# Earlier query projections in layer 1, a later memset and cycling tail banks in a two-layer attention and token-mixer kernel

## The chip, the cores and the metric

The kernel runs on one core of a Trainium2 chip. The metric is device time in microseconds (us) of one execution. A core has a matrix engine (TensorE, PE; its weight loads are shown as PEld), VectorE (DVE), ScalarE (ACT), GpSimd (POOL) and a queue engine (SyncE, SP), which run their own instruction lists in order and wait for each other through semaphores. Matrix results land in eight PSUM banks; everything else lives in SBUF.

## What is computed

Two layers, each an attention block and a token-mixing MLP, with layer normalisation before each and a residual after each, on a sequence of S = 2048 tokens of D = 640 with H = 32 heads of 20, and F = 1536 hidden units that mix along the sequence. Both layers use the same weights.

```python
def _A_ref(x, wqkv, wo):
    B, S, D = x.shape
    H = 32
    Dh = D // H
    qkv = (lambda x, *d: x.transpose(*d))((x @ wqkv).reshape(B, S, 3, H, Dh), 2, 0, 3, 1, 4)
    q, k, v = qkv[0], qkv[1], qkv[2]
    scores = jnp.einsum("bhqd,bhkd->bhqk", q, k) * (Dh ** -0.5)
    p = _softmax(scores, axis=-1)
    o = jnp.einsum("bhqk,bhkd->bhqd", p, v)
    return (lambda x, *d: x.transpose(*d))(o, 0, 2, 1, 3).reshape(B, S, D) @ wo

def _B_ref(x, w1, b1, w2, b2):
    B, S, D = x.shape
    h = _layernorm(x, axis=-1)
    u = jnp.einsum("bsd,sf->bdf", h, w1) + b1
    u = _gelu(u)
    y = jnp.einsum("bdf,fs->bds", u, w2) + b2
    return (lambda x, *d: x.transpose(*d))(y, 0, 2, 1)

x = A_x
x = x + _A_ref(_layernorm(x, axis=-1), A_wqkv, A_wo)
x = x + _B_ref(_layernorm(x, axis=-1), B_w1, B_b1, B_w2, B_b2)
x = x + _A_ref(_layernorm(x, axis=-1), A_wqkv, A_wo)
x = x + _B_ref(_layernorm(x, axis=-1), B_w1, B_b1, B_w2, B_b2)
return x
```

## The kernel before

**Tiling.** Tokens go in 16 tiles of 128 and in four blocks of 512 (`tb` for keys, `qb` for queries). Heads go in eight groups `g` of four. A *unit* is one query block, one head group and one key tile; its four heads are four *chunks* of 128 x 512 scores. A layer has 512 units and 2048 chunks. Scores S = K Q (L703) are written by PE into a 3-bank and a 2-bank PSUM tile in turn, ScalarE takes their exponential (L773, forms of 1536 and 1024 columns) into P, and PE sums P with the values into `acc` (L1326). The value tile `Vaug` holds, for each key tile and head, 20 values and a column of ones that gives the softmax denominator.

**Helping ScalarE.** Some chunks have their exponential taken by VectorE and GpSimd instead (L563, L661, L593, L597, L644, L614, L616), in pairs, through the PSUM bank Dt. In layer 0 this starts early (`ve_early = True`), in layer 1 only once all tokens have been fed in.

**The order.** Python code plans the whole kernel: it keeps model clocks for PE, VectorE and ScalarE (`pem`, `dvm`, `acm`), decides step by step what PE does next, and writes the instructions of PE, VectorE, ScalarE and GpSimd in that order. So a changed priority at one place moves instructions in all that follows. Between score rows PE does *fills* out of a queue sorted by priority, lowest number first (`add_fill`, `next_fill`): T (transposes of a normalised tile, L1225), K and Q projections (L1177), V projections (L1201), y (second matmul of the mixer of the layer before, L1685, in layer 1), O (output projection) and M (first matmul of the mixer, L1068). A fill takes one of the banks `misc` and `Dt`, and is copied or added out by VectorE, or by ScalarE at the very start (the helper lines L366 and L370 to L372). Where there is no fill, PE multiplies zeros (L762). `fed` marks the fills that must be done before the second phase of a layer opens.

**Feeding.** After the four transposes of a token block, `t_fill` queues its K projections (priority `when(g, tb) - 4`) and, for block 0, its Q projections. `EQ` holds the query blocks 0 and 1, whose units may run early, on whatever keys are there. For block 1 the four Q projections of the first four groups are queued after the transposes of that block, at L1247 to L1249. `base[1]` is 16, so that their priorities are 28, 36, 44 and 52.

**Start of layer 0.** `TokenFeed.begin` zeroes the values' padding on ScalarE (`zero_values`), and then submits a VectorE memset of the column of ones (L1546), with the model time `e + 5.0` as its earliest. VectorE meanwhile normalises the first six token tiles (statistics L886 to L893, `veps` L901, a power on GpSimd L903, `h_bf` L907); PE transposes four of them, ScalarE copies them to `hh`, and V, K and Q of block 0 follow.

**End of a layer.** When the last unit's sums are out, the 3-bank and 2-bank score tiles become the accumulators `sums` of the last two token tiles' output: ScalarE puts the residual into them (L955), M fills that have been begun or fit into 1.3 us of model time are done, the last projection is added (L960), and the M fills that are left follow. Their banks come from `tail_alloc`: first misc, then Dt, then the third bank of the first score tile; there is no fourth. Their adds into the hidden rows (L1076) on VectorE are kept in the list `held` once L960 is out, and are forced after statistics of the two tiles (L980 to L993). Then come the two normalised tiles (L995, L999) and the mixer (`mixer_head`: um L1753, its add L1756, GELU L1759, then ya and yb).

Of the kernel before, what the change touches and what calls it, by code (L numbers as in the profile page):

```python
# [25 lines left out]
DH = 20  # L26
# [55 lines left out]
def kernel(  # L82
# [12 lines left out]
    nc = tc.nc  # L95
# [16 lines left out]
    def pe(inst):  # L112
        tc.chain_iter_dep("pe_order", inst.ins)
        return inst
# [77 lines left out]
    Vv = Vaug[:, 0:NKT * H * VW].rearrange("p (k h c) -> p k h c", k=NKT, h=H)  # L192
# [26 lines left out]
    def get_QT(st, qb):  # L219
        if qb not in st.QTq:  # L220
            st.QTq[qb] = qtp.tile([128, NG, 512], BF16, name="QTq")
        return st.QTq[qb]

    def attention(st, x_in_ap, x_mid, uacc_l, feed, feed_stack):
# [10 lines left out]
        def s_tile(w):  # L235
            return pp[f"s{w}"].tile([128, w, 512], F32, name="S")
# [38 lines left out]
        misc = Bank(lambda: pp["misc"].tile([128, 512], F32, name="misc"))  # L275
        Dbank = Bank(lambda: pp["dt"].tile([128, 512], F32, name="Dt"))
# [47 lines left out]
        held = []  # L324
# [38 lines left out]
        def copy_on(eng, out_ap, in_ap, scale=None):  # L363
            if eng is acm:
                if scale is None:
                    nc.scalar.copy(out=out_ap, in_=in_ap)  # L366
                else:
                    nc.scalar.mul(out=out_ap, in_=in_ap, mul=scale)
            elif scale is None:
                nc.vector.tensor_copy(out=out_ap, in_=in_ap)  # L370
            else:
                nc.vector.tensor_scalar_mul(out=out_ap, in0=in_ap, scalar1=scale)  # L372
# [15 lines left out]
        base = [0.0]  # L388
# [782 lines left out]
        def proj_fill(kind, g, tb, prio, ready, gate=None, fed=False):  # L1171
            wpad, key = (wk_pad, ("K", g, tb)) if kind == "K" else (wq_pad, ("Q", tb, g))
            scale = None if kind == "K" else q_scale
            mms = []
            for dt_ in range(NDT):
                def mm(t, dt_=dt_):
                    pe(nc.tensor.matmul(t[:, :], lhsT=wpad[:, dt_, g, :], rhs=hT[:, dt_, tb * 512:(tb + 1) * 512],  # L1177
                                        start=(dt_ == 0), stop=(dt_ == NDT - 1)))
                mms.append(mm)

            def evac(t, end, eng):
                dst = KT[:, g, tb * 512:(tb + 1) * 512] if kind == "K" else get_QT(st, tb)[:, g, :]
                copy_on(eng, dst, t[:, :], scale)

            def after(end):
                kready[key] = end + DVE_TO_PE
            add_fill(key, prio, mms, evac, 512, ready=ready, after=after, act=0.6, gate=gate, fed=fed)
# [26 lines left out]
        def when(g, tb):  # L1214
            return base[tb] + per_g[tb] * g if g < EG else place[(0, g)] + 4.0 * tb

        def t_fill(tt, h_bf, ready, done):
            tb = tt // 4

            def view(t):  # L1220
                return t[:, :].bitcast(BF16)[:, 0:D].rearrange("p (a b) -> p a b", a=NDT)
            mms = []
            for dt_ in range(NDT):
                def mm(t, dt_=dt_):
                    pe(nc.tensor.transpose(view(t)[:, dt_, :], h_bf[:, dt_ * 128:(dt_ + 1) * 128], ident[:]))  # L1225
                    if dt_ == NDT - 1:
                        done()
                mms.append(mm)

            def evac(t, end, eng):  # L1230
                copy_on(eng, hT[:, :, tt * 128:(tt + 1) * 128], view(t))

            def after(end):
                tready[tt] = at = end + DVE_TO_PE
                v_fill(tt, 0, feed.wv_early, when(0, tb) + tt % 4 - 1, at, fed=True,
                       gate=(lambda: len(tready) >= 4) if tb == 0 else None)
                if all(4 * tb + i in tready for i in range(4)):
                    for g in list(range(EG)) + rest:
                        gate = feed.gate_late if g >= EG else None
                        owner = next((qb for qb in EQ if part_at[qb] <= g < part_at[qb] + part_rows), None)  # L1240
                        if owner is not None:
                            gate = lambda owner=owner: feed.gate_late() and not any(qg[0] == owner for qg in early_left)
                        proj_fill("K", g, tb, when(g, tb) - 4, max(at, cx.w_at.get((0, g), at + 1.0)), gate=gate, fed=g < EG)
                        if tb == 0:
                            proj_fill("Q", g, 0, when(g, 0) - 4, max(at, cx.w_at.get((1, g), at + 1.0)),
                                      gate=feed.gate_late if g >= EG else None, fed=g < EG)
                    if tb in EQ and tb > 0:  # L1247
                        for g in range(EG):
                            proj_fill("Q", g, tb, base[tb] + 16.0 + 8.0 * g - 4, at, fed=True)  # L1249
                if len(tready) == NT and NQB > 1:  # L1250
                    enqueue_qproj(1)
            add_fill(("T", tt), when(0, tb) - 6 + 0.1 * (tt % 4), mms, evac, D, ready=ready, after=after, wave=0.1,
                     cells=0.25, cost=0.48, act=0.7, fed=True)

# [158 lines left out]
        cx = Ctx()  # L1413
        cx.w_at = {}
        for k_, v_ in dict(dvm=dvm, acm=acm, pem=pem, Proc=Proc, submit=submit, ln_proc=ln_proc, t_fill=t_fill,
                           add_fill=add_fill, when=when, v_fill=v_fill, proj_fill=proj_fill, enqueue_qproj=enqueue_qproj,
                           kready=kready, vready=vready, base=base, rest=rest, tready=tready, s_start=s_start, KT=KT,
                           Dbank=Dbank, misc=misc, spare=spare, warm_bank=warm_bank, acc_free=acc_free, pe_wave=pe_wave,
# [33 lines left out]
        sums = [s_tile(w)[:].rearrange("p a b -> p (a b)") for w in (3, 2)]  # L1452
        for t in sums:
            zero_wave(t[:, 0:512], True, True)
            zero_wave(t[:, 512:D], True, True, HALF / 2, D - 512)
        tail_banks = [sums[0][:, 1024:1536], None, None]

        def tail_alloc():
            bank = tail_banks.pop()
            return bank if bank is not None else Dbank.alloc() if len(tail_banks) == 1 else misc.alloc()  # L1460
        room = pem["t"] + 1.3
        while fs["cur"] is not None or (fill_queue and pem["t"] < room):
            fill_step(tail_alloc)
# [7 lines left out]
    class TokenFeed:  # L1471
        groups = 4
        early_qbs = (0, 1)
        ve_early = True
        act_helps = True
        act_free = 0.0
        warm_until = 5.6
# [28 lines left out]
        def begin(self, cx):  # L1506
# [36 lines left out]
            def zero_values(e):  # L1543
                nc.scalar.memzero(Vv[:, :, :, DH:VW])
                nc.scalar.memzero(Vv[:, :, 4 * self.groups, 0:32 - VW])
                cx.submit(cx.Proc(2.6, [(0.49, lambda e: nc.vector.memset(Vv[:, :, :, DH:DH + 1], 1.0), 0.0)], e + 5.0))  # L1546
            cx.submit(cx.Proc(1.4, [(1.35, zero_values, -0.06),
                                    (0.2, lambda e: nc.scalar.memzero(Vaug[:, NKT * H * VW:]), -0.06)] +
                              [(1.0, lambda e, i=i: nc.scalar.memzero(pads(i, 1)), -0.06) for i in range(2)],
# [43 lines left out]
    class MixFeed:  # L1593
        groups = 4
        early_qbs = (0, 1)
        ve_early = False
        act_helps = True
        act_free = 0.0
        warm_until = 0.0
# [239 lines left out]
    with ExitStack() as a_stack:  # L1839
# [3 lines left out]
        feed = TokenFeed(feed_stack)  # L1843
        attention(st0, A_x[0], xd[0], uacc[0], feed, feed_stack)
    with ExitStack() as a_stack:
# [3 lines left out]
        feed = MixFeed(feed_stack, xd[0], xd[1], st0.ua)  # L1849
# [33 lines left out]
```

## Time and profile before

| what | us |
|---|---|
| three runs, median (lowest to highest) | 1754.15 (1754.06 to 1754.17) |
| the profiled execution | 1754.05 |
| its span, first to last instruction | 1752.3 |
| ScalarE busy in the span | 1665.0 (95%) |
| PE busy | 1677.7 (96%) |
| VectorE busy | 1534.9 (88%) |
| GpSimd busy | 592.0 (34%) |

The engines' busy shares are close to each other, and PE's includes products of zeros and repeated score matmuls that nothing waits for. The chain that ended last, followed back from the end, has ScalarE with 50% of the span, PE with 25% and issue time with 22%. A view by stage says more than these averages: the two attentions lie at 16 to 817 us and 853 to 1681 us; between them and behind them stand the mixers. A row of a timeline gives start, duration, engine, line, operation, output and input tile, shape and count, and in brackets the idle time of the engine before it with what ended it. Durations of neighbouring instructions of ScalarE and VectorE overlap a little, so that the distance from start to start is what one costs.

### The profile page before, as it was taken

The page shows a single profiled execution, that of the slowest core. Times are in us where ns is not written, and L with a number is a line of the kernel's source. Part 1 is how long each engine was busy: PE and PEld are TensorE (multiplying, and loading weights), DVE is VectorE, ACT ScalarE, POOL GpSimd, SP SyncE. Part 2 cuts the span into 40 slices and gives each one's busy share as a digit, 9 for nine tenths or more (in the row PEclk, how much of TensorE's full clock was granted, in tenths as well). Part 3 has the DMA queues.
Part 4 walks back from the last instruction along what each step waited for, and adds up shares of the span by engine and source line. Part 5 has one row for each costly group of instructions (what it writes and reads, how often), then busy time and mean ns, then how long its engine had stood idle before and what let it go on. Part 6 is the DMA issues. An engine that isn't in the chain of part 4 may idle for free.

```text
span 1752.3 us, 43289 instructions
## 1 busy us (share of the span) xinstructions
PE 1677.7 (96%) x17891; PEld 663.4 (38%) x17891; DVE 1534.9 (88%) x2491; ACT 1665.0 (95%) x1498; POOL 592.0 (34%) x936
## 2 busy tenths in 40 slices
PE   8999999999999999999999999999999999999999
PEld 3333333333333344444434433233333333444455
DVE  7789999999999999998543469999999999999973
ACT  8999999999999999999779999999999999999970
POOL 2243443353544343332000023434434443434310
PEclk9999999999999999999999999999999999999999
DMA  4020000000122010133322100001001220101445
GB/s 117 9 24 10 1 2 2 24 24 2 35 66 82 25 47 3 39 97 97 125 69 75 65 11 1 1 2 43 20 2 61 82 76 6 62 3 40 120 122 178
DMA packets 103014, 81.87 MB, mean 47 GB/s; under 512 B 50976, under 2 KB 87456, under 8 KB 102816
## 3 DMA queue, kind: packets, MB, share of 16 engines
q1 hardware_dynamic: 97280, 71.22, 13.5%
q0 software_dynamic: 5536, 7.88, 1.5%
q8 instruction: 140, 2.29, 0.5%
q14 instruction: 58, 0.48, 0.1%
HBM read 55.48 MB, written 23.59 MB: 45 GB/s over the span
## 4 chain that ended last, share of the span: by engine, by line
ACT 50%; PE 25%; issue 22%; DVE 2%; DMA 1%; POOL 0%; SPq 0%; ACTq 0%; DVEq 0%
ACT P L773 50%; PE S L703 7%; PE acc L1326 4%; PE misc L1068 2%; PE ya L1766 2%; PE misc L1177 2%; PE acc L762 2%; PE um L1753 1%; PE Dt L1177 1%; PE ya L1775 1%; PE yb L1766 1%; DMA w2s<-in_B_w_dram 1%; PE misc L1117 0%; PE misc L1685 0%; PE misc L1201 0%
## 5 line engine op out<-in xcount | busy, mean ns | idle before, releaser
L773 ACT ACTIVATE P<-S 128x1536 bf16<-128x1536 f32 (+1 forms) x1430 | 1617.4, 1369 | 13.5 <-PE S L703 13.0
L703 PE MATMUL S<-QTq,KT 32*128 32x512 bf16 (+1 forms) x4449 | 575.6, 337 | 60.9 <-ACT P L773 44.4
L661 POOL TENSOR_SCALAR ey<-ew 128x512 f16<-128x512 uint16 x516 | 320.6, 621 | 689.6 <-DVE et L597 306.4
L703 PEld LDWEIGHTS <-KT 32*128 32x128 bf16 x5127 | 229.6, 91 | 524.6 <-issue 497.0
L563 DVE TENSOR_SCALAR ew<-Dt 128x512 int32<-128x512 f32 x524 | 357.0, 681 | 22.3 <-PE Dt L703 14.8
L1326 PE MATMUL acc<-P,Vaug 128*32 128x512 bf16 (+1 forms) x4442 | 363.3, 343 | 0.3 <-DVE Vaug L370 0.3
L762 PE MATMUL acc<-zr,zw 128*32 128x512 bf16 x4256 | 328.1, 382 | 1.2 <-POOL zr L155 1.2
L597 DVE SCALAR_TENSOR_TENSOR et<-ey,ew 128x1024 int16<-128x1024 f16 x262 | 325.6, 1243 | 2.8
L644 POOL TENSOR_SCALAR Pd<-ew 128x512 int16<-128x512 int16 x317 | 196.8, 627 | 161.6 <-DVE et L597 42.4
L703 PE MATMUL Dt<-QTq,KT 32*128 32x512 bf16 (+1 forms) x678 | 201.4, 333 | 0.0
L593 DVE TENSOR_TENSOR ey<-ey 128x1024 f16<-128x1024 f16 x262 | 188.3, 719 | 1.4 <-POOL ey L661 0.3
L1326 PEld LDWEIGHTS <-Vaug 128*32 128x32 bf16 x5120 | 102.7, 94 | 175.4 <-issue 161.4
L762 PEld LDWEIGHTS <-zw 128*32 128x32 bf16 x4476 | 111.5, 96 | 97.9 <-issue 52.5
L616 DVE SCALAR_TENSOR_TENSOR Pd<-ew,et 128x1024 int16<-128x1024 int16 (+1 forms) x134 | 134.6, 1005 | 0.6
L614 DVE TENSOR_TENSOR Pd<-Pd,et 128x1024 int16<-128x1024 int16 (+1 forms) x189 | 121.8, 645 | 5.8 <-POOL Pd L644 3.8
L903 POOL TENSOR_TENSOR rstd<-veps,mhalf 128x1 f32<-128x1 f32 x60 | 49.4, 824 | 224.6 <-DVE veps L901 197.2
L1326 PE MATMUL acc<-Pd,Vaug 128*32 128x512 bf16 (+1 forms) x678 | 102.9, 336 | 1.4 <-DVE Pd L614 1.2
L1177 PE MATMUL misc<-hh,wq_pad 128*128 128x512 bf16 x290 | 84.0, 383 | 0.0
L1068 PEld LDWEIGHTS <-w1st 128*128 128x128 bf16 x672 | 52.9, 97 | 58.2 <-issue 45.3
L1177 PE MATMUL misc<-hh,wk_pad 128*128 128x512 bf16 x255 | 74.0, 383 | 0.0
L1068 PE MATMUL misc<-x1last,w1st 128*128 128x320 bf16 x384 | 73.0, 302 | 0.0
L1117 PE MATMUL misc<-wo_pad,attnT 128*128 128x320 bf16 x384 | 72.3, 302 | 0.2 <-DVE xin L1129 0.2
(145 smaller groups left out, 1180.4 us busy)
## 6 DMA issues: line engine op xcount, KB each, us to landing
w2s<-in_B_w_dram SPq DMA_DIRECT2D x16, 768.0 KB
uacc<-ustg POOLq DMA_DIRECT2D x24, 320.0 KB, 2.6
x1in<-xd SPq DMA_DIRECT2D x24, 320.0 KB
w1st<-in_B_w_dram SPq DMA_DIRECT2D x24, 256.0 KB
xd<-x2s SPq DMA_DIRECT2D x16, 320.0 KB
xin<-xd SPq DMA_DIRECT2D x16, 320.0 KB
w1st<-in_B_w_dram SPq DMA_DIRECT2D x24, 192.0 KB
xd<-x1s SPq DMA_DIRECT2D x12, 320.0 KB
```

Of the source, the lines that this page charges most:

```text
L563: nc.vector.tensor_scalar(out=w[:, slot, :], in0=Dt[:, :], scalar1=127.0 * FIX, scalar2=0.0, op0=ALU.add, op1=ALU.max)
L593: nc.vector.tensor_tensor(out=y, in0=y, in1=y, op=ALU.mult)
L597: nc.vector.scalar_tensor_tensor(out=box["t"][:, 0:512 * k], in0=ve_y.pop(p)[:, 0:512 * k], scalar=MANT_C * MANT_K ** 2, in1=frac, op0=ALU ...
L616: nc.vector.scalar_tensor_tensor(out=bits, in0=whole[:, lo:hi], scalar=128.0, in1=t, op0=ALU.mult, op1=ALU.add)
L644: after_vector(nc.gpsimd.tensor_scalar(out=bits, in0=whole, scalar1=128.0, scalar2=0.0, op0=ALU.mult, op1=ALU.add))
L661: return engine.tensor_scalar(out=out_ap, in0=in_ap, scalar1=MANT_K / FIX, scalar2=-MANT_K * MANT_S, op0=ALU.mult, op1=ALU.add)
L703: pe(nc.tensor.matmul(out_ap[:, c0:c0 + w], lhsT=KT[32 * j:32 * j + 32, g, kt * 128:(kt + 1) * 128], rhs=get_QT(st, qb)[32 * j:32 * j + 32 ...
L762: pe(nc.tensor.matmul(bank[32 * j:32 * j + 32, 0:w], lhsT=zw[:], rhs=zr[:, :, 0:64].to_broadcast([128, w // 64, 64]), start=start, stop=st ...
L773: nc.scalar.activation(out=P[:, 0:ncs, :].rearrange("p a b -> p (a b)"), in_=St[:, 0:ncs, :].rearrange("p a b -> p (a b)"), func=ACT.Exp, ...
L1068: pe(nc.tensor.matmul(t[:, 0:w], lhsT=w1_of[(p, ft)][:, sti, :], rhs=rows_in[sti][:, c0:c1], start=(sti == 0), stop=(sti == n_in - 1)))
L1177: pe(nc.tensor.matmul(t[:, :], lhsT=wpad[:, dt_, g, :], rhs=hT[:, dt_, tb * 512:(tb + 1) * 512], start=(dt_ == 0), stop=(dt_ == NDT - 1)))
L1326: pe(nc.tensor.matmul(acc[32 * j:32 * j + 32, a0:a0 + w], lhsT=Vaug[:, (kt * H + hh_) * VW:(kt * H + hh_) * VW + 32], rhs=P[:, slot, c0:c0 ...
```

## The change

Three edits. In layer 1 (`MixFeed`, `early_q = -5.5`) the Q projections of block 1 get the priorities -5.50 to -5.47 instead of 28 to 52; layer 0 (`early_q = None`) keeps its numbers. The memset of the column of ones may start 3 us of model time later. `tail_alloc` hands out misc, Dt and the third score bank in turn without end, and from the fourth on it first drains the oldest held add.

```diff
                     if tb in EQ and tb > 0:
                         for g in range(EG):
-                            proj_fill("Q", g, tb, base[tb] + 16.0 + 8.0 * g - 4, at, fed=True)
+                            proj_fill("Q", g, tb, base[tb] + (8.0 * g + 12.0 if feed.early_q is None else 0.01 * g + feed.early_q),
+                                      at, fed=True)
...
-        tail_banks = [sums[0][:, 1024:1536], None, None]
+        tail_banks = [misc.alloc, Dbank.alloc, lambda: sums[0][:, 1024:1536]]
+        tail_used = [0]
 
         def tail_alloc():
-            bank = tail_banks.pop()
-            return bank if bank is not None else Dbank.alloc() if len(tail_banks) == 1 else misc.alloc()
+            if tail_used[0] >= len(tail_banks) and len(held) > 1:
+                force(held.pop(1))
+            tail_used[0] += 1
+            return tail_banks[(tail_used[0] - 1) % len(tail_banks)]()
...
         ve_early = True
+        early_q = None
...
-                cx.submit(cx.Proc(2.6, [(0.49, lambda e: nc.vector.memset(Vv[:, :, :, DH:DH + 1], 1.0), 0.0)], e + 5.0))
+                cx.submit(cx.Proc(2.6, [(0.49, lambda e: nc.vector.memset(Vv[:, :, :, DH:DH + 1], 1.0), 0.0)], e + 8.0))
...
         ve_early = False
+        early_q = -5.5
```

## The prediction

> **What bounds the kernel now.** I read the stage windows first, then ScalarE's groups by shape, then the ordered timelines of ScalarE and VectorE at the three places that the change touches: the start of layer 0, the start of layer 1, the end of layer 1. Busy time by stage (columns: stretch; length; PE, PEld, DVE, ACT, POOL busy with instruction counts; clock; DMA):
>
> ```profile
> 16.00:816.80 800.80, 768.12 (x8476) 291.59 (x8477) 757.22 (x1200) 800.24 (x707) 311.06 (x482) 1.00 0.12 32
> 816.80:853.30 36.50, 34.73 (x309) 19.64 (x303) 27.81 (x65) 23.21 (x32) 4.38 (x8) 1.00 0.59 193
> 853.30:900.60 47.30, 45.73 (x343) 19.95 (x342) 21.12 (x43) 36.56 (x34) 1.65 (x3) 1.00 0.24 76
> 900.60:1027.00 126.40, 122.04 (x954) 49.53 (x954) 50.21 (x105) 126.40 (x112) 4.40 (x8) 1.00 0.17 52
> 1027.00:1681.40 654.40, 628.37 (x7168) 239.74 (x7167) 635.39 (x982) 654.12 (x579) 263.94 (x416) 1.00 0.11 35
> ```
>
> ScalarE (ACT) is busy 800.24 of 800.80 us in layer 0's attention and all but 0.3 us of layer 1's from 900.6 on. So inside an attention time is saved only by giving ScalarE fewer exponentials; outside, by starting it earlier or finishing sooner behind it. Its exponentials:
>
> ```profile
> L773 ACT ACTIVATE P<-S 128x1536 bf16<-128x1536 f32 x714 | 1128.0, 1580 | 4.1 <-PE S L703 3.6 <-PE Dt L703 0.2
> L773 ACT ACTIVATE P<-S 128x1024 bf16<-128x1024 f32 x714 | 828.1, 1160 | 9.4 <-PE S L703 9.4
> ```
>
> The means hold an overlap with the next one, but their difference, 0.42 us for 512 columns, does not. With 354 wide and 353 narrow ones filling 800.24 us, a narrow one costs (800.24 - 354*0.42)/707 = 0.92 us of ScalarE and a wide one 1.34; a 512-wide one, a step below, 0.50.
>
> ScalarE in the first part of layer 1:
>
> ```profile
> 883.44 7.37 ACT L773 ACTIVATE P<-S 128x1024 bf16<-128x1024 f32 x7 [8.34 <-PE S L703]
> 892.16 7.38 ACT L773 ACTIVATE P<-S 128x1536 bf16<-128x1536 f32 x7 [1.35 <-PE S L703]
> ```
>
> It ran out of scores three times: 8.34 us, 1.35 us and, at 900.59, 1.05 us.
>
> VectorE in the first microseconds, and behind the last exponential of layer 1:
>
> ```profile
> 8.01 0.15 DVE L901 TENSOR_SCALAR veps<-mv 128x1 f32<-128x1 f32 x1
> 10.06 0.48 DVE L1546 MEMSET Vaug<- 128x512 bf16 x1 [1.90 <-ACT hh L366]
> 10.14 0.55 DVE L907 TENSOR_SCALAR h_bf<-x0in,mv,rstd 128x640 bf16<-128x640 bf16 x1
> 10.61 0.48 DVE L886 BATCH_NORM_STATS2 bnst<-x0in 128x6 f32<-128x320 bf16 x1
> ```
>
> ```profile
> 1682.98 0.45 DVE L834 STREAM_TRANSPOSE attnT<-T 128x256 bf16<-128x256 bf16 x1
> 1683.35 0.45 DVE L1076 TENSOR_TENSOR KT<-misc,KT 128x320 f32<-128x320 f32 x1
> 1684.87 0.49 DVE L1076 TENSOR_TENSOR KT<-misc,KT 128x320 f32<-128x320 f32 x1 [1.06 <-PE misc L1068]
> 1685.48 0.90 DVE L980 BATCH_NORM_STATS2 bnst<-S 128x6 f32<-128x320 f32 x2
> ```
>
> VectorE sits 1.90 us ahead of the column's memset, with the normalisation of the fourth tile queued behind it. At the other end, two leftover sums (L1076) stand between the last transposed attention tile and the statistics that the rest of the layer waits for.
>
> **The change, part by part.** The kernel is laid out by a planner, so I compared the instruction orders of the two built programs and priced what moves.
>
> *Exponentials.* VectorE takes two more score chunks in each layer (280 to 282, 244 to 246). In layer 0 ScalarE's list loses a 1536-wide one and gains a 512-wide one: -1.34 + 0.50 = -0.84 us. In layer 1 it has two fewer of 1024, one fewer of 512, one more of 1536: -1.84 - 0.50 + 1.34 = -1.00 us. Both lie on the path. The some forty extra operations on VectorE and GpSimd do not: of ScalarE's idle time before its exponentials, 13.5 us, 13.0 is ended by a score matmul.
>
> *Start of layer 1.* The order is the same up to the transposes of tokens 512 to 1023, so the 8.34 us gap stays. Behind them stood one K and one V projection ahead of five score matmuls; now nine matmuls of two Q projections stand there, one fewer (0.22 us), so the 1.35 us gap becomes 1.15. Four Q fills then open 16 units on keys already present, each four chunks, 1.8 us of ScalarE (4 * 800.24/1768), and the later double row of scores behind the K fills, where the 1.05 us gap was, is gone from the order. Sum -1.25 us; bounds -2.4 (both go) and 0 (other gaps of this size replace them). What is late next is K and V of the second block; the 29 us of open units cover them. Without that cover a K fill costs 1.08 us on PE (chain of waits), a copy of 0.69 and a score row of about 0.4: 2.2 us each time.
>
> *Memset.* It goes behind the statistics of tiles 4 and 5, next to the first V copy. If the 1.90 us leave with it, the fourth h_bf runs at 8.85 (its rstd ended at 8.79) instead of 10.14. But the input of tile 4 landed only at 10.43, so the statistics start at 10.5 instead of 10.61, and the memset's 0.40 us (0.48 less the 0.08 that neighbours overlap) now lie in the busy stretch. In the new order and at the spacings of the old rows: memset 12.37 (1.89 behind the first statistics), V copy 12.77, fifth h_bf 13.13, veps 13.49, KT's copy 13.61 (14.03 before), sixth h_bf 14.28 (its rstd takes until 14.23), QTq's copy 14.64 to 15.32, against 15.31. PE's V projection in front of the first scores then ends at 15.2 instead of 15.6, and the first scores wait for QTq: 15.37 against 15.54. I take -0.2 us. Below: the chain follows the earlier projections alone and gains as much as the fourth tile's transposes and K, about -1.1. Above: the 1.90 us belong to the memset wherever it stands. Its one semaphore wait, on ScalarE's first zeroing, was met at 3.2 us, so the stall is not explained, and this end counts: 15.3 + 1.9 for QTq, +1.8 in all.
>
> *End of layer 0.* No sums are left over, before or after; only the last softmax tile is narrower. 0, bounds +-0.5 (half a score tile). The 36.5 us up to layer 1's first exponential hold the same instructions.
>
> *End of layer 1.* Here two more leftover sums of six matmuls are outside the attention: two whole ones now stand ahead of the last output projection (one before), two behind (one before). When a fourth bank is asked for, the new allocator drains the oldest held sum, so that VectorE's order has four L1076 adds ahead of the statistics L980, against two, and the fourth waits for matmuls that stand behind the projection. Counted from the last exponential (1681.39): first add 1.96 as before; second sum on PE at 2.46; third 0.81 later, 3.27; projection 0.81 later, 4.08 (3.27 before); the fourth sum 1.09 behind, 5.17; its add 1.02 later, 6.19; the statistics 0.41 behind, 6.60. Before: 1685.48 - 1681.39 = 4.09. So +2.5 us, and nothing hides it: from L980 to the first um matmul (1689.30) each step waits for the one before, and then PE is busy 59.23 of 63.00 us. Bounds 0 (the adds move off the path) and +3.
>
> Sum: -0.84 - 1.00 - 1.25 - 0.2 + 0 + 2.5 = -0.8 us. The profiled execution has a span of 1752.3 and 1.75 around it, 1754.05; less 0.8, 1753.25. The shown median is 0.10 above it: 1753.3.
>
> *Zero waves.* 20 fewer (80 of 4440 such matmuls): nothing while ScalarE is the bound, as long as PE keeps its clock, 1.00 in every stretch above and in every slice:
>
> ```profile
> PEclk9999999999999999999999999999999999999999
> ```
>
> **Rivals.**
> (a) *The memset carries its stall along.* For: the wait is unexplained and stands directly at it. Against: its neighbour started only 0.08 us behind, as if both had been held. Startup +1.8 instead of -0.2: total +1.2, 1755.3.
> (b) *The tail is free.* For: the rows that these adds complete are read only by the last um matmuls, so nothing else needs them early. Against: VectorE takes its list in order. -3.3 in all, 1750.8; with the startup's -1.1 too, 1749.9.
> (c) *ScalarE starves again, the slower side.* Q moved ahead means K and V of the second block, and with them the mixer fills and the transposes of the third, come later; the units run out a second time, as at 875. For: a gap of 8.34 us exists where the same happened. Against: 16 units are 29 us. It decides when ScalarE's idle time from 853 to 1027 passes the 10.7 us of before; two K-fill waits of 2.2 make +4.4 and lose the 1.25: total about +4.9, 1759.0.
> (d) *The clock drops where filler was taken away.* It decides from a PE pause far longer than any here: the longest of the trace is 0.81 us, at 1683. Priced on the stretch from 900.6: 25 us of it hold 24.1 us of matmuls (122.04 of 126.40), at half rate 48.3, so +23, 1776. [...]
>
> **How the numbers follow.** Forecast 0.56, (a) 0.14, (b) 0.15, (c) 0.13, (d) 0.02. The likeliest is the forecast, 1753.3; its own range, from the startup's and the gap's bounds, is 1751.5 to 1755.0. The stated range goes from (b) with the better startup, 1749.9, to above (a) with a little new idling, 1756.5, and leaves out (c) and (d) and little else. A measurement of this kernel tells 0.2% from no change, 3.5 us: under 1750.6 lie nearly half of (b) and a few lucky forecasts, 0.12; over 1757.7 nearly all of (c), (d) and the worst of (a), 0.14; between them 0.74.
>
> **What would show it.** Memset: first exponential at 15.8 (not 16.0 or 17.8), and no idle VectorE ahead of L1551. Layer 1: the 8.34 us gap still there, the second 1.15, no third. Tail: four L1076 adds ahead of L980, which starts 6.6 us behind the last exponential. ScalarE's attention stretches shorter by 0.84 and, from the first exponential of layer 1, 2.25 us. Wrong if a new ScalarE gap over 1 us stands inside an attention, or if L980 keeps its 4.1 us.

## The result, and the profile after

The changed kernel took 1758.05 us (median of 21 runs, 1756.25 to 1758.32) against 1754.15 for the kernel before (21 runs, 1754.01 to 1755.41): a ratio of 1.0019, 95% interval 1.0012 to 1.0026. The runs of the changed kernel fall into two groups, and with one exception the granted clock tells them apart: 7 had a mean clock of 1.000 and a median of 1756.69 (one of them, 1758.07, lies with the other group), 14 had 0.999 and a median of 1758.15. The profiled execution is of the first group: 1756.51 us with a span of 1754.6, 2.3 us more than the span before. So the loss has two parts, 2.3 us that the profile shows in place, and about 1.5 us that most executions lose on top.

The windows of the changed kernel's profile, by stage (columns as before: stretch; length; PE, PEld, DVE, ACT, POOL busy with counts; clock; DMA):

```profile
17.10:818.50 801.40, 765.43 (x8427) 291.39 (x8427) 763.60 (x1205) 799.68 (x707) 317.27 (x496) 1.00 0.12 32
818.50:855.00 36.50, 34.74 (x309) 19.52 (x298) 27.83 (x65) 23.23 (x32) 4.36 (x8) 1.00 0.58 193
855.00:900.00 45.00, 43.33 (x321) 18.72 (x320) 20.35 (x41) 35.24 (x32) 1.64 (x3) 1.00 0.25 80
900.00:1025.00 125.00, 120.87 (x931) 49.22 (x934) 53.48 (x110) 125.00 (x111) 4.38 (x8) 1.00 0.18 53
1025.00:1680.96 655.96, 631.32 (x7206) 244.15 (x7206) 637.89 (x990) 655.61 (x580) 268.28 (x423) 1.00 0.11 35
1680.96:1754.60 73.64, 67.44 (x537) 38.08 (x530) 32.60 (x63) 14.66 (x19) 1.10 (x2) 0.99 0.57 178
```

The boundaries are the first and last exponentials of the two layers, with two cuts inside layer 1's attention, at 900 and 1025. The table sets these stretches beside those of before, in us, each from the start of its first exponential to the end of its last:

| stretch | before | after | difference | forecast |
|---|---|---|---|---|
| start to the first exponential | 15.97 | 17.14 | +1.17 | -0.2 |
| layer 0's exponentials | 800.84 | 801.38 | +0.54 | -0.84 |
| to layer 1's first exponential | 36.44 | 36.42 | 0 | 0 |
| layer 1's exponentials | 828.13 | 826.02 | -2.11 | -2.25 |
| last exponential to the end | 70.91 | 73.64 | +2.73 | +2.5 |

Layer 1 and the tail came as forecast, the start and layer 0 did not. ScalarE in the timeline of the changed kernel, at its first exponential, at two new gaps and at the start of layer 1:

```profile
17.14 1.45 ACT L773 ACTIVATE P<-S 128x1536 bf16<-128x1536 f32 x1 [3.84 <-PE S L703]
...
138.30 4.62 ACT L773 ACTIVATE P<-S 128x1536 bf16<-128x1536 f32 x4 [0.77 <-PE S L703]
...
885.33 7.37 ACT L773 ACTIVATE P<-S 128x1024 bf16<-128x1024 f32 x7 [8.56 <-PE S L703]
893.91 11.40 ACT L773 ACTIVATE P<-S 128x1536 bf16<-128x1536 f32 x10 [1.21 <-PE S L703]
```

In layer 1 the third gap, of 1.05 us, is gone, and the second shrank from 1.35 to 1.21. In layer 0 a gap of 0.77 us is new, and another of 0.42 at 231; before there was one of 0.30 at 698.

The first of the two new gaps, on VectorE and TensorE:

```profile
136.76 0.47 DVE L370 CAST Vaug<-misc 128x320 bf16<-128x320 f32 x1
137.29 0.38 PE L1177 MATMUL misc<-hh,wq_pad 128*128 128x512 bf16 x1 [0.92 <-DVE Vaug L370]
```

VectorE and TensorE in the first microseconds of the changed kernel, and VectorE at its end:

```profile
11.65 0.21 DVE L893 BATCH_NORM_AGGREGATE mv<-bnst 128x2 f32<-128x12 f32 x1
13.72 0.48 DVE L1551 MEMSET Vaug<- 128x512 bf16 x1 [1.87 <-ACT wq_pad L1564]
13.83 0.70 DVE L370 CAST Vaug<-misc 128x320 bf16<-128x320 f32 x1
14.58 1.24 PE L1177 MATMUL misc<-hh,wq_pad 128*128 128x512 bf16 x5 [2.54 <-DVE Vaug L370]
```

```profile
1683.09 0.45 DVE L1076 TENSOR_TENSOR KT<-misc,KT 128x320 f32<-128x320 f32 x1
1684.61 0.49 DVE L1076 TENSOR_TENSOR KT<-misc,KT 128x320 f32<-128x320 f32 x1 [1.07 <-PE misc L1068]
1685.43 0.49 DVE L1076 TENSOR_TENSOR KT<-Dt,KT 128x320 f32<-128x320 f32 x1 [0.32 <-PE Dt L1068]
1687.38 0.49 DVE L1076 TENSOR_TENSOR KT<-S,KT 128x320 f32<-128x320 f32 x1 [1.47 <-PE S L1068]
1687.79 0.89 DVE L980 BATCH_NORM_STATS2 bnst<-S 128x6 f32<-128x320 f32 x2
```

The memset has its idle time ahead of it at the new place too, 1.87 us against 1.90. Behind it the value copy is late, the bank misc comes free late, and TensorE's first query projection waits 2.54 us. The longest pause of before, once TensorE had started, was 1.06 us:

```profile
8.77 0.44 PE L1225 MATMUL misc<-ident,h_bf 128*128 128x128 bf16 x5 [1.06 <-ACT hh L366]
```

At the end four adds stand ahead of the statistics L980, which start 6.83 us behind the last exponential.

### The profile page after: what moved, and what is told of

The parts are those of the page before. It is cut to its first block, busy times and chain, and to the rows that moved or that the text cites. A ratio compares the mean times of both kernels' runs of the same rounds, so it can differ in the third digit from the quotient of the medians.

```text
span 1754.6 us, 43238 instructions
## 1 busy us (share of the span) xinstructions
PE 1676.2 (96%) x17838; PEld 667.2 (38%) x17838; DVE 1547.6 (88%) x2510; ACT 1663.2 (95%) x1496; POOL 602.5 (34%) x957
## 4 chain that ended last, share of the span: by engine, by line
ACT 51%; PE 24%; issue 21%; DVE 3%; POOL 1%; DMA 0%; ACTq 0%; DVEq 0%; POOLq 0%; SPq 0%
ACT P L773 50%; PE S L703 7%; PE acc L1327 3%; PE ya L1772 2%; PE acc L762 2%; PE misc L1068 2%; PE misc L1177 2%; PE um L1759 1%; PE misc L1117 1%; PE ya L1781 1%; PE yb L1772 1%; DVE et L597 1%; DVE ew L563 1%; PE Dt L1177 0%; PE Dt L703 0%
## 5 line engine op out<-in xcount | busy, mean ns | idle before, releaser
L597 DVE SCALAR_TENSOR_TENSOR et<-ey,ew 128x1024 int16<-128x1024 f16 x264 | 330.4, 1251 | 3.3
L644 POOL TENSOR_SCALAR Pd<-ew 128x512 int16<-128x512 int16 x337 | 207.3, 619 | 163.8 <-DVE ey L593 45.0
L614 DVE TENSOR_TENSOR Pd<-Pd,et 128x1024 int16<-128x1024 int16 (+1 forms) x200 | 130.6, 653 | 5.6 <-POOL Pd L644 2.5
L616 DVE SCALAR_TENSOR_TENSOR Pd<-ew,et 128x512 int16<-128x512 int16 (+1 forms) x127 | 123.7, 974 | 0.4
L1177 PE MATMUL misc<-hh,wk_pad 128*128 128x512 bf16 x275 | 79.6, 383 | 0.0
```

The lines of the kernel that those rows point to most:

```text
L597: nc.vector.scalar_tensor_tensor(out=box["t"][:, 0:512 * k], in0=ve_y.pop(p)[:, 0:512 * k], scalar=MANT_C * MANT_K ** 2, in1=frac, op0=ALU ...
L614: nc.vector.tensor_tensor(out=bits, in0=bits, in1=t, op=ALU.add)
L644: after_vector(nc.gpsimd.tensor_scalar(out=bits, in0=whole, scalar1=128.0, scalar2=0.0, op0=ALU.mult, op1=ALU.add))
```

## The experiments

Theory A, after these profiles: the memset costs its 1.9 us wherever it stands, and at the new place TensorE stands still for so long behind it, 2.54 us, that in most executions (14 of 21, mean clock 0.999) its clock is halved for a while. Against it stood that the lost clock belongs to layer 1 or the tail, and that the 1.9 us belong to the place.

### Which edit costs what

`undo_memset` puts the memset back and keeps the rest; `undo_q` takes only the early queries back.

```diff
-                cx.submit(cx.Proc(2.6, [... nc.vector.memset(Vv[:, :, :, DH:DH + 1], 1.0) ...], e + 8.0))
+                cx.submit(cx.Proc(2.6, [... nc.vector.memset(Vv[:, :, :, DH:DH + 1], 1.0) ...], e + 5.0))
```

> The memset of the ones goes back to e + 5.0; the early query projections and the three-bank tail stay. Layer 0 is then the program of before, instruction for instruction, and layer 1 that of the changed kernel. Theory A (the moved memset carries a stall of its own of 1.9 us and, by holding the value copy behind it, opens the 2.54 us pause of TensorE that costs the clock about 0.1% of the run): first exponential back at 16.0, layer 0's exponentials over 800.8, layer 1 2.1 shorter and the tail 2.7 longer than before: 1754.7 us, granted clock 1.000, no group of runs 1.5 us higher. Rival B (the clock is lost in the changed layer 1 or in its tail): most runs at 1756.3, clock 0.999. Rival C (the query projections themselves cost): over 1756 with the clock at 1.000.

Measured: 1755.07 (1754.96 to 1756.18; ratio to before 1.0006, 0.9997 to 1.0015). Nine of 11 runs had the clock at 1.000 and a median of 1755.06; the first exponential stood at 15.90 and layer 0's took 800.84, as before. That is 0.4 above the 1754.7 expected. The profiled execution is one of the two with a clock of 0.999, and its half-rate window stands in layer 1, at 887 us; but a later profile with the same two layers and full clock throughout (`mem_two_w8`) also has 826.3 us of exponentials in layer 1, 0.3 more than the changed kernel's 826.02: from 1203 us on the same exponentials in the same order take 477.04 us in place of 476.51. Why is open. The move of the memset, with the other order of layer 0 that it brings, thus costs 3.0 us of the 3.9. What is left, the earlier queries and the tail, is 0.9 above before at the median, with 1 still inside the interval.

```diff
-        early_q = -5.5
+        early_q = None
```

> Only the query projections of layer 1 go back to their old due time; the memset stays late. Layer 0 is that of the changed kernel, layer 1 that of before. Theory A: the startup and layer 0 keep their +1.2 and +0.5, so 1754.15 + 1.7 = 1755.9 with the clock at 1.000 in the smaller part of the runs, and 1757.4 with the clock at 0.999 in the larger part; layer 1's third gap of about 1 us is back and statistics L980 begin about 4.1 us behind the last exponential. Rival B (clock lost in the changed layer 1 or its tail): nearly all runs at 1755.9 or below, clock 1.000.

Measured: 1757.34 (1755.96 to 1758.53; ratio 1.0018, 1.0009 to 1.0026), nine of 11 runs below a clock of 1.000. Layer 1 and its tail are those of before here (exponentials 828.35 us, tail 70.9), so the clock is lost in the startup or layer 0; and the tail's +2.7, like layer 1's -2.1, comes with the earlier queries and not with the cycling of the banks by itself, which is still in this kernel. The profiled execution is one that lost it. Its windows, laid in steps of 3.41 us:

```profile
11.84:15.25 3.41, 0.84 (x5) 0.30 (x4) 1.54 (x6) 1.55 (x4) 0.65 (x2) 1.00 0.01 2
15.25:18.66 3.41, 3.41 (x14) 1.04 (x11) 2.26 (x5) 0.23 (x1) 0.44 (x1) 0.50 0.55 137
18.66:22.07 3.41, 3.41 (x19) 1.22 (x18) 2.24 (x7) 3.41 (x4) 0.00 (x0) 1.00 1.02 319
```

and TensorE in the same execution:

```profile
14.71 1.80 PE L1177 MATMUL misc<-hh,wq_pad 128*128 128x512 bf16 x5 [2.57 <-DVE Vaug L370]
16.30 1.54 PE L1201 MATMUL Dt<-x1last,hh 128*128 128x320 bf16 x5
```

The first column of busy time is TensorE's, the last but two the clock. A window with 0.84 us of work is followed by one at a clock of 0.50, and the next is at 1.00 again. In it the five matmuls of the query projection take 1.80 us in place of 1.24, the first exponential comes at 18.43 in place of 17.14. One such window makes a mean clock of 0.999 over 1754 us, as the slower group has it; no profile of the changed kernel itself was taken in that group. The stretch at half rate is 3.41 us long. Whether the same program has one differs from one execution to the next: 14 of 21 of the changed kernel and nine of 11 here had the lower clock.

### Filling the pause

`fill_pause` puts 28 multiplications by zero ahead of the first query projection of layer 0; all other instructions keep their order.

```diff
+                    if feed.early_q is None and key == ("Q", 0, 0) and dt_ == 0:
+                        for j in range(28):
+                            pe(nc.tensor.matmul(warm_bank()[32 * (j % 4):32 * (j % 4) + 32, 0:512], lhsT=zw[:],
...
```

> 28 multiplications by zero into the unused warm-up bank are put into TensorE's pause ahead of the first query projection; every other instruction on every engine is that of the changed kernel. Theory A (the 2.54 us pause is what drops the clock in most executions): all runs fall into the lower group, 1756.3 to 1757.0, clock 1.000; the first exponential stays at 17.1. Rival B (the clock is lost elsewhere): most runs stay at 1758.1, clock 0.999. If the extra multiplications run past the value copy, the first exponential is up to 0.5 us later, and so is the end.

```profile
12.03 1.70 PE L1179 MATMUL acc<-zr,zw 128*32 128x512 bf16 x28
14.67 1.24 PE L1182 MATMUL misc<-hh,wq_pad 128*128 128x512 bf16 x5 [0.95 <-DVE Vaug L370]
```

In TensorE's timeline the pause is down to 0.95 us. Measured: 1756.98 (1756.24 to 1757.85; ratio 1.0016, 1.0007 to 1.0025), the clock at 1.000 in 10 of 11 runs, against 7 of 21 in the changed kernel. The products that nobody reads made the kernel 1.1 us faster at the median. The times spread more than expected, up to 1757.6 at full clock.

### What the memset costs

`ones_twice` issues the memset twice.

> The changed kernel with the memset issued twice in a row, nothing else changed. Theory A (the stall is the memset's own): two idle stretches of 1.9 us on VectorE, the value copy 2.3 to 2.4 us later than 13.8, first exponential at 19.4, total 1758.6 to 1760.5. Rival D (VectorE waits there for something that happens once): one stretch of 1.9 us, the second memset follows at once, the value copy at 14.2 to 14.3, first exponential at 17.6, total 1756.9 to 1758.6.

VectorE's timeline:

```profile
14.21 0.48 DVE L1551 MEMSET Vaug<- 128x512 bf16 x1 [1.87 <-ACT wq_pad L1565]
16.68 0.48 DVE L1552 MEMSET Vaug<- 128x512 bf16 x1 [1.99 <-issue]
16.78 0.70 DVE L370 CAST Vaug<-misc 128x320 bf16<-128x320 f32 x1
```

The second one stands 2.47 us behind the first, with nothing to wait for. So the cost is the instruction's own: about 2.4 us for one, of which its row shows 0.48, at its end. TensorE's pause grew to 5.29 us and cost two half-rate windows:

```profile
12.47:15.88 3.41, 0.00 (x0) 0.00 (x0) 0.48 (x1) 0.98 (x3) 0.31 (x1) 1.00 0.00 1
15.88:19.29 3.41, 1.75 (x5) 0.64 (x5) 2.26 (x6) 0.00 (x0) 0.55 (x1) 0.50 0.11 32
19.29:22.70 3.41, 3.41 (x14) 1.04 (x13) 1.58 (x3) 0.95 (x1) 0.00 (x0) 0.50 0.84 217
```

The first exponential came at 21.75 where 19.4 was expected, and the four runs took 1760.28 to 1761.06, median 1760.56 (ratio 1.0033, 1.0019 to 1.0048): the theory had the stall right and the clock's second window missing.

`ones_copy` writes the same column, at the same place, as a copy from a tile of ones.

```diff
-... nc.vector.memset(Vv[:, :, :, DH:DH + 1], 1.0) ...
+... nc.vector.tensor_copy(out=Vaug[:, 0:NKT * H * VW].rearrange("p (a c) -> p a c", c=VW)[:, :, DH:DH + 1],
+                          in_=zr[:, :, 0:1].to_broadcast([128, NKT * H, 1])) ...
```

> The memset of the ones is replaced by a copy of ones from a tile that holds them, in the same place with the same wait; the rest is the changed kernel's program. Theory A (the stall belongs to the memset): no idle time of 1.9 us ahead of the copy, the value copy about 1.9 us earlier (12.0), TensorE's pause under 1 us, first exponential 15.3 to 16.0, total 1754.6 to 1755.4 with the clock at 1.000 throughout. Rival D (the stall belongs to the place: something VectorE waits for or that runs then on another engine): the copy too starts at 13.7 behind 1.9 us of idle time, first exponential 17.1, total 1756.5 to 1758.1.

```profile
11.12 0.49 DVE L886 BATCH_NORM_STATS2 bnst<-x0in 128x6 f32<-128x320 bf16 x1 [1.78 <-DMA x0in<-in_A_x_dram]
...
13.02 1.29 DVE L1551 COPY Vaug<-zr 128x512 bf16<-128x512 bf16 x1
13.90 0.71 DVE L370 CAST Vaug<-misc 128x320 bf16<-128x320 f32 x1
```

No idle time stands ahead of the copy any more, as theory A has it; but the copy itself costs 0.88 us from start to start. From the last statistic to the value copy it is 1.0 us (12.89 to 13.90) in place of 2.2 (11.65 to 13.83). In this execution the fifth token tile landed later, at 11.12 in place of 9.87, which took the 1.2 us away again: the first exponential stayed at 17.22. The median over all runs is 1756.12 (1755.70 to 1757.15; ratio 1.0011, 1.0002 to 1.0020), 1.9 below the changed kernel and 0.7 to 1.5 above what was expected: right on the mechanism, wrong on what the replacement costs. Most of the 1.9 is the clock, which was full in 9 of 11 runs with a pause of 1.56 us; among runs at full clock the gain is 0.6 (1756.07 against 1756.69). Its layer 0 has the gaps of 0.78 and 0.42 us too, so these come from the new plan and not from the stall.

Why did the same 1.9 us cost nothing at the old place? `before_pool` is the kernel before with the column written by GpSimd:

```diff
-                cx.submit(cx.Proc(2.6, [... nc.vector.memset(Vv[:, :, :, DH:DH + 1], 1.0) ...], e + 5.0))
+                nc.gpsimd.memset(Vv[:, :, :, DH:DH + 1], 1.0)
```

> The kernel before with the ones on GpSimd in place of VectorE's memset; nothing else differs. If the memset's 1.9 us lie under the wait for the fifth token tile: no idle stretch ahead of a memset, in its place 1 to 2 us of idle time that a DMA ends, first exponential at 15.6 to 16.5 and 1753.8 to 1754.7. If they were on the path: first exponential at 14.7 and 1752.9.

```profile
9.10 0.45 DVE L907 TENSOR_SCALAR h_bf<-x0in,mv,rstd 128x640 bf16<-128x640 bf16 x1 [0.66 <-POOL rstd L903]
10.51 0.49 DVE L886 BATCH_NORM_STATS2 bnst<-x0in 128x6 f32<-128x320 bf16 x1 [0.97 <-DMA x0in<-in_A_x_dram]
```

With the memset gone VectorE waits for the fifth token tile instead, until 10.51, and the first exponential is at 15.90, 0.07 earlier. Median 1753.90 (1753.03 to 1755.92; ratio 0.9998, 0.9990 to 1.0007). At its old place the memset lay under a load; behind the statistics of that tile nothing covers it. The cover is only as long as the load: a later run with the ones on GpSimd (`pool_nd_warm`), in whose profile the fifth token tile's statistics start at 9.65, has its first exponential at 15.04, 0.9 earlier.

### What the tail costs

`room0` lets no new leftover fill start ahead of the last projections; `mem_room0` does so with the memset at its old place, `pool_room0` with the ones on GpSimd.

```diff
-        room = pem["t"] + 1.3
+        room = pem["t"]
```

> In the tail of layer 1 no leftover fill of the MLP is started ahead of the last output projections L960 (the room of 1.3 us is set to 0); the startup and layer 0 are the changed kernel's. Theory A (the tail's +2.7 us is the two whole fills that TensorE runs ahead of L960, and their adds ahead of L980 on VectorE): one add fewer by two ahead of L980 (2 in place of 4), L980 starts about 5.0 us behind the last exponential in place of 6.8, the end comes 1.6 to 2.2 us earlier: 1754.3 to 1754.9 with the clock at 1.000 and 1755.9 to 1756.5 where it drops at the startup. Rival B (the fills have to be done anyway and only come later, behind the statistics): L980 is earlier but the end is not, 1756.3 to 1758.1 as in the changed kernel.

> The memset back at e + 5.0 and the tail's room at 0, the early query projections kept. If the three parts add: 1755.07 as measured with the memset back, less 1.6 to 2.2 in the tail: 1752.9 to 1753.5, which is below the kernel before by 0.6 to 1.2. If the leftover fills only move behind the statistics: 1755.1.

> As the run before, but the ones are written by GpSimd ahead of its first power, and VectorE has no memset of the column; every other instruction on every engine has the same order. Theory A (VectorE stood 1.9 us for its memset, and this bounds the startup): no idle stretch of 1.9 us on VectorE; the fourth tile's normalization starts at 8.85, behind its power on GpSimd, in place of 10.1, and the first exponential is up to 1.3 us earlier, at 14.7, total 1.3 below the run with the memset. Rival D (the loads or ScalarE's copies bound the startup anyway): first exponential stays at 15.9, the total is the same.

Measured: 1758.45, 1755.55 and 1755.71 (ratios 1.0022, 1.0008 and 1.0005, intervals 1.0013 to 1.0030, 0.9999 to 1.0017, 0.9996 to 1.0014). The first is no faster than the changed kernel, the second slower than `undo_memset` by 0.5. With the ones on GpSimd the first exponential stood at 16.56 in the profile, behind a fifth token tile whose statistics started only at 11.18, so the run says nothing against the loads as the bound of the startup. L980 did start earlier, 5.81 us behind the last exponential, not 5.0; the end did not come earlier. Two things took the gain. The sums um now waited for the three adds that had moved behind the statistics, and the planner, with more fills left over, had cut the closing waves of zeros from 10 to 4, so that TensorE stood idle. Its timeline and its windows in `room0`:

```profile
1687.46 1.05 PE L762 MATMUL acc<-zr,zw 128*32 128x512 bf16 x16
1691.20 1.36 PE L1759 MATMUL um<-hh,KT 128*128 128x512 bf16 x8 [2.70 <-DVE KT L1076]
```

```profile
1688.79:1692.20 3.41, 1.00 (x7) 0.59 (x8) 2.62 (x9) 1.51 (x2) 0.55 (x1) 1.00 1.11 344
1692.20:1695.61 3.41, 3.15 (x13) 1.52 (x12) 2.58 (x4) 2.23 (x3) 0.00 (x0) 0.50 1.12 326
```

The same event again, at the other end of the kernel. `mem_room0_warm` restores the 10 waves and changes nothing else:

```diff
-        for _ in range(max(4, WARM_WAVES - 4 * rest_fills[0])):
+        for _ in range(max(10, WARM_WAVES - 4 * rest_fills[0])):
```

> The run with the old memset and the tail's room at 0, but with the 10 closing waves of multiplications by zero (40 of them) that the changed kernel has at the end of layer 1, in place of 4; nothing else differs. Theory A (the fewer waves left TensorE idle for 2.70 us ahead of the MLP's first sums, which halved the clock for one window of 3.4 us): the clock is 1.000 in the stretch behind the tail, the run is 1.7 us below the earlier one in nearly all executions, at 1754.5 or 1754.7 (the pause was there in all of them, the earlier median 1755.55 had some without the drop), and um still starts 10.2 us behind the last exponential, because the three adds behind the statistics hold it. Rival (the half-rate stretch there has another cause): again 0.8 of the clock at 1692 to 1700 and 1755.5.

Measured: 1754.73 (1754.58 to 1755.80; ratio 1.0002, 0.9994 to 1.0011), full clock in 10 of 11 runs against one of 11, um 10.19 us behind the last exponential. The half-rate window cost 0.8 here and not 1.7; that the stage has waits which absorb part of it is a guess.

`mem_nd_warm` and `pool_nd_warm` keep the fills ahead of the projection, and leave out the drain that forces the fourth add ahead of the statistics (again with 10 waves, and with the memset at its old place or on GpSimd):

```diff
-            if tail_used[0] >= len(tail_banks) and len(held) > 1:
-                force(held.pop(1))
```

> The old memset, the early query projections, and the three-bank tail without the drain that forces a held add before a bank is taken again; 10 closing waves as in the changed kernel. Only one add (of bank S) moves on VectorE, from ahead of statistics L980 to behind them. Theory A (the tail's cost is the fourth add, which waits for the fourth fill): L980 starts 4.9 to 5.0 us behind the last exponential in place of 6.8, um 9.2 to 9.4 in place of 10.6, the end 1.2 to 1.4 earlier than 1755.07: 1753.7 to 1753.9. Rival B (the adds only move behind the statistics and hold um there): L980 is earlier, um is not, and the time stays at 1755.0.

> As the run before with the ones on GpSimd in place of VectorE's memset. If the loads of the fifth and sixth token tile set the startup (VectorE waits for them until 10 to 11 anyway), the time is the same within 0.4: 1753.5 to 1754.1. If VectorE's 1.9 us ahead of the memset set it, 1752.4 to 1752.6.

```profile
1685.35 0.49 DVE L1076 TENSOR_TENSOR KT<-Dt,KT 128x320 f32<-128x320 f32 x1 [0.32 <-PE Dt L1068]
1687.32 0.90 DVE L980 BATCH_NORM_STATS2 bnst<-S 128x6 f32<-128x320 f32 x2 [1.48 <-PE S L1068]
```

Measured: 1754.68 and 1755.31 (ratios 1.0003 and 1.0006, intervals 0.9994 to 1.0012 and 0.9996 to 1.0015), no better than the run before. The second had a clock of 0.999 in 7 of its 11 runs. The fourth add was out of the way, and L980 came 6.44 us behind the last exponential in place of 6.83: it then waited for TensorE's fill into bank S. The fill lies in columns 1024 to 1535 of that tile, the sums that L980 reads in the first 640, but the wait is on the tile. So the add was the last of two waits with nearly one end. `mem_two` and `pool_two` cycle misc and Dt alone:

```diff
-        tail_banks = [misc.alloc, Dbank.alloc, lambda: sums[0][:, 1024:1536]]
+        tail_banks = [misc.alloc, Dbank.alloc]
```

> Old memset, early query projections, and a tail whose leftover fills cycle two banks (misc and Dt) without the drain, so that none goes into the third part of bank S; the number and order of the fills and adds is that of the run without the drain. Theory E (the statistics L980 read bank S and are held until the fill that was last written into it, though that lies beside the sums): L980 starts 5.0 to 5.2 us behind the last exponential in place of 6.4, in line behind the third add, and the sums um 9.0 to 9.3 in place of 10.2; 1753.5 to 1753.9. Theory F (it is the number of leftover fills: TensorE and VectorE have the same work to do before um in any order): L980 is earlier, um is not, 1754.6 as without the drain.

> As mem_two with the ones written by GpSimd. Under theory E, with loads that land as in most runs, 0 to 0.9 below mem_two: 1752.6 to 1753.9, with single executions up to 1755.5 where the loads land late or the clock drops for a window in layer 1. Under theory F 1753.7 to 1755.3, as the earlier variant with GpSimd.

```profile
1685.26 0.49 DVE L1076 TENSOR_TENSOR KT<-Dt,KT 128x320 f32<-128x320 f32 x1 [0.32 <-PE Dt L1068]
1685.87 0.90 DVE L980 BATCH_NORM_STATS2 bnst<-S 128x6 f32<-128x320 f32 x2
```

With the same number of fills L980 starts 5.08 us behind the last exponential. Medians 1753.79 and 1753.68 (ratios 0.9998 and 0.9997, intervals 0.9989 to 1.0007 and 0.9989 to 1.0006). Taking the third bank out of the cycle is worth 0.9 to 1.0 us among the runs at full clock. What is left of the tail's loss over before: one whole fill more ahead of L960, 0.8 us, and TensorE's ten waves, which now ended exactly where um began:

```profile
1687.87 2.34 PE L762 MATMUL acc<-zr,zw 128*32 128x512 bf16 x40
1690.14 1.26 PE L1757 MATMUL um<-hh,KT 128*128 128x512 bf16 x8
```

`mem_two_w8` and `pool_two_w8` have 8 waves:

> mem_two with 8 closing waves of multiplications by zero in place of 10 in layer 1; nothing else differs. Theory G (the waves hold um): um starts 8.9 us behind the last exponential in place of 9.35, right behind ScalarE's normalized tile, the end 0.4 to 0.45 earlier: 1753.2 in the executions with full clock. Rival H (the add behind the statistics, which ends at the same moment, holds um): um stays at 9.3, TensorE stands idle 0.4 us ahead of it, 1753.6 in the executions with full clock.

> As mem_two_w8 with the ones written by GpSimd. Theory G: 0 to 0.9 below mem_two_w8, lowest runs at 1752.6 to 1753.0. Rival H: as pool_two, lowest runs at 1753.4.

Measured: 1753.36 (1753.17 to 1754.71) and 1753.84 (1752.71 to 1754.87), against 1754.12 for before; ratios 0.9995 (0.9987 to 1.0004) and 0.9997 (0.9988 to 1.0006). um started 8.93 us behind the last exponential. `mem_two_w8` is the best kernel of the study: 8 of its 11 runs lie below the fastest of before's 21 (1753.92), though at 0.8 us below at the median the interval still holds 1, so that faster than before is not shown. Among the runs at full clock alone the medians go from 1755.06 (`undo_memset`) by 1754.72 (`mem_room0_warm`), 1754.65 (`mem_nd_warm`) and 1753.74 (`mem_two`) to 1753.34, against 1754.10 for before. GpSimd's version has the lowest single runs and a wider spread; in the profiles of the kernels with the ones on GpSimd the first exponential moves between 15.04 and 16.56 with the landing of the fifth tile.

## Why the prediction was wrong

*Memset, the step that failed.* "I take -0.2 us": measured +1.17, with the 1.87 us standing at the new place. The step's upper bound of +1.8 and rival (a) were the right mechanism; that the profile shows only 1.17 goes with the fifth token tile, which landed about 0.6 us earlier in it (its statistics start at 9.87) than in the trace of before. Rival (a) was put down at 0.14 because its neighbour followed only 0.08 us behind, "as if both had been held". But its neighbour follows this memset as closely wherever it stands: 0.11 in the changed kernel, 0.10 behind the second one of `ones_twice`. The closeness said nothing for or against. And the old trace showed why the stall had been nearly free: the tile that the next statistics read landed only at 10.43. I drew from it that little was to be gained, and not that the stall would lose this cover at the new place.

*The clock, rival (d).* Its condition, "a PE pause far longer than any here", came true through (a), which I had priced alone. (The longest pause of before was misread: 1.06 us at 8.77, not 0.81.) Pauses of 2.57 us in `undo_q` and 2.70 in `room0` were followed by half rate. Its price of +23 us was wrong: the half is what the profiles show, a clock of 0.50, but no run shows it for the 25 us of the price. It lasted 3.41 us in `undo_q` and 6.82 in `ones_twice`, and the two groups of the changed kernel's runs lie 1.5 us apart. As alternatives (a) and (d) gave 1755.3 and 1776; they came together and gave 1758.05, above the range. The forecast's own range was not what its bounds make, either: they make 1751.3 below, and above 1754.6 or, with the stall, 1756.6, where 1751.5 and 1755.0 stand; the result lies outside both.

*Exponentials of layer 0, the second step that failed.* -0.84 forecast, +0.54 measured. ScalarE's busy time fell by 0.56 (799.68 against 800.24), but it idles 1.16 us more in the attention (1.72 of 801.40, against 0.56 of 800.80). I had said that the extra operations on VectorE do not lie on the path. At 137.29 TensorE waits 0.92 us for VectorE's value copy, which stands behind VectorE's steps of a helped exponential, and ScalarE waits 0.77 behind it. The gap at 231 looks different: ahead of its scores TensorE multiplies zeros, from 229.3 to 231.1. The two gaps are there in every profile with this layer 0 and in none with the old plan, so they come with the new order; no run takes single operations of it back. This was an error of 1.4 us, as large as that of the start.

*Start of layer 1.* Right: 8.56, 1.21, no third gap; the stretch -2.11 against -2.25, and gone again in `undo_q`.

*End of layer 1.* Right in size, +2.73 against +2.5, and four adds, L980 at 6.83 against 6.60. The reason was half of it: without the fourth add the wait for bank S takes over 0.4 us earlier. Rival (b), a free tail, fell: the adds behind the statistics held um in `room0`.

In the profiled execution the forecast of -0.8 missed +2.3 by 3.1: 1.4 at the start, 1.4 in layer 0, 0.1 in layer 1 and 0.2 in the tail. The half-rate window adds 1.5 in two runs of three. `undo_memset` takes back the start, the clock and layer 0's order at once; how its 3.0 us divide among them is read from the profiles.

## What to carry to other kernels

Count an instruction's unexplained idle time (here 1.90 us, and 1.87 at the new place) as its own until a run shows otherwise; ask what covered it at the old place, and move it under another wait or to an idle engine. A pause of TensorE can have a second price behind its length (in `undo_q`, 3.41 us at a clock of 0.50 behind a pause of 2.57), so that rivals which cause each other must be priced together; and cutting products of zeros can cost more than it saves (`mem_room0`, with 4 waves, took 0.8 us more than `mem_room0_warm` with 10). A bank lent out beside data that another engine reads tied the two together here, even where their columns do not meet: VectorE stood 1.48 us for it in `mem_nd_warm`, and not in `mem_two`.

## What the runs showed of the hardware

- VectorE's memset of 512 single bf16 elements per partition, one in each run of a strided pattern, costs 2.47 us from start to start (`ones_twice`; 2.34 from the end of the row ahead of it to its own end in the changed kernel), where its row shows 0.48. A copy to the same column costs 0.88 (`ones_copy`). The two memsets of 480 uint32 zeros, in runs of 6, at 0.93 and 1.43 us stand 0.50 apart with 0.46 in the row. Whether the pattern, the type or the value makes the difference, no run separates.
- The stretches at a clock of 0.50 were 3.41 us long in `undo_q` (15.25 to 18.66), `undo_memset` (887.24 to 890.65), `room0` (1692.20 to 1695.61) and `mem_room0_warm` (99.12 to 102.53), and 6.82 in `ones_twice` (15.88 to 22.70). In the 3.41 us ahead of them TensorE was busy 0.00 us in `ones_twice`, 0.84 in `undo_q` and 1.00 in `room0`; once at half rate, a window with 1.75 was followed by another (`ones_twice`). In `mem_room0` the 4 us from 1688 hold 1.30 us of work, and the clock over the 8 us behind them is 0.79; in `pool_room0` they hold 1.33, and the clock is 0.77 in them and 0.90 behind. A pause of 2.57 us in `undo_q` was followed by half rate, one of 2.54 in the profile of the changed kernel was not (clock 1.00 from 9.17 to 19.41), though 14 of that kernel's 21 runs had the lower clock. What decides between executions is not shown.
- Busy time alone does not tell. In `undo_memset` a window with 2.55 us of work in 25 matmuls at the start of layer 1 was followed by half rate too, and in `mem_room0` the clock is 0.65 from 888 to 892, where `pool_room0` has 1.00; in `mem_room0_warm` the half-rate window stands in layer 0, behind one with 2.71. In the changed kernel's profile a stretch of 3.41 us with 1.42, from 12.59, was followed by full clock. What is counted there stays open. Windows of `undo_memset`:

```profile
883.83:887.24 3.41, 2.55 (x25) 1.35 (x23) 1.90 (x4) 3.41 (x4) 0.00 (x0) 1.00 0.69 252
887.24:890.65 3.41, 3.41 (x20) 0.90 (x17) 0.49 (x1) 3.36 (x4) 0.00 (x0) 0.50 0.02 5
```
